# The second layer of an ffn by Strassen's seven products, with buffers turned in place, in a fused attention and ffn kernel

## The chip, the cores and the metric

The kernel runs on one core of a Trainium2 chip. The metric is the device time of one execution in microseconds; the kernel before takes 1520.41 us (median of 3 runs, 1520.29 to 1524.58). All arithmetic is in fp32.

## The reference

Attention with a threshold for 8 batches of 8 heads, 576 tokens and 64 columns a head; its output, 4608 rows of 512 columns, goes into a feed-forward network (ffn) with two first-layer weights whose products are multiplied element by element.

```python
scores = scale * np.matmul(q, k.transpose(0, 1, 3, 2))        # q, k, v: (8, 8, 576, 64)
thresh = np.max(scores, axis=-1, keepdims=True) - tau
scores = np.where(scores >= thresh, scores, -1000000000.0)
scores = scores - np.max(scores, axis=-1, keepdims=True)
attn = np.exp(scores)
attn = attn / (np.sum(attn, axis=-1, keepdims=True) + 1e-09)
x = np.matmul(attn, v)           # then (B, H, S, D) -> (B*S, H*D) = (4608, 512)
a = x @ w_a                      # w_a, w_b: (512, 1536), float64 in memory
b = x @ w_b
return (a * b @ w_out)           # w_out: (1536, 512)
```

## The kernel before

The work of attention is cut into 160 units: a pair of heads with 128 rows of each (or, at the end of a pair, the last 64 rows of both). The ffn is cut into 18 blocks of 256 rows. TensorE's program interleaves them: after the scores of a unit come pieces of the current ffn block, counted in columns, so that TensorE has work while VectorE and ScalarE do the softmax. All engines run their instructions in the order written. Every matmul uses a quarter of the array (64 rows by 64 columns), so that four run side by side; `r` picks the half of the rows and `c` the half of the columns.

Scores and softmax of a unit (`banks` gives a PSUM tile of two banks; there are four):

```python
    def scores(i, u):
        ...                                    # matmuls into sc[0], sc[1], 128x576 each
        for j in range(n):
            c = slice(j, j + 1)
            nc.vector.tensor_reduce(mx[:, c], sc[j], axis=AX.XY, op=ALU.max)
            nc.gpsimd.tensor_scalar(bias[:, c], mx[:, c], e_nscale, None, op0=ALU.mult)
        nc.gpsimd.tensor_scalar(thr[:, 0:n], mx[:, 0:n], cut, None, op0=ALU.subtract)

    def weigh(i, u):
        for j, s in enumerate(sc):
            w = work.tile([P, S], FP32, tag="w", bufs=W_BUFS, name="w")
            nc.scalar.activation(..., s, AF.Exp, bias=bias[:, j:j + 1], scale=e_scale)
        for j, s in enumerate(sc):
            nc.vector.scalar_tensor_tensor(out=wv, in0=s, scalar=thr[:, j:j + 1], in1=wv,
                op0=ALU.is_ge, op1=ALU.mult, accum_out=sums[:, j:j + 1])
```

The weights are normalised by ScalarE, turned in 32x32 blocks by VectorE into another tile `tb`, and written to a scratch buffer in HBM and read back turned (`wT`). q and k are loaded into tiles `qm`, `km` and turned by VectorE into `qT`, `kT`:

```python
    def turn_blocks(i, u):
            for j, w in enumerate(ws):
                nc.vector.transpose(tb[...], w.rearrange("p (n e) -> p n e", e=Q))
            for g in range(G):
                nc.sync.dma_start(swap[...], tb[g * Q:(g + 1) * Q])
    def prep(i, name):
        mT = work.tile([P, S], FP32, tag=name + "T", bufs=HP, name=name + "T")
        nc.vector.transpose(mT, m.rearrange("p n e -> p (n e)"))
```

The weighted values go into the tile `xT`; GpSimd copies its upper and lower halves crosswise into `xS`:

```python
    def exchange(x, xs, hp, c0, c1, engine):
        for r in range(2):
            engine.tensor_copy(xs[r * D:(r + 1) * D, hp, c0:c1], x[(1 - r) * D:(2 - r) * D, hp, c0:c1])
    def join(out, lo, hi):
        nc.scalar.copy(out, lo)
        nc.vector.tensor_tensor(out, out, hi, op=ALU.add)
```

One block of the ffn (`HALF` is 256, `NF` 12, `DM` 512, `H` 8); each `yield` is a place where attention may come in between:

```python
    def ffn(xT, what):
        for f, c0, c1 in steps:                     # first layer: 6 steps of 256 hidden columns
            for w in (wa_sb, wb_sb):
                pab = banks(c1 - c0, "pab")
                for k in range(H):
                    for r in range(2):
                        for c in range(2):
                            nc.tensor.matmul(pab[c * D:(c + 1) * D, r],
                                             w[rows, f // n, k, fs + c * D:fs + (c + 1) * D], moving,
                                             start=(k == 0), stop=(k == H - 1))
                    yield ...
                if w is wa_sb:
                    nc.scalar.copy(ht, pab)
                else:
                    nc.vector.tensor_tensor(ht, ht, pab, op=ALU.mult)
        for u in range(2):                          # second layer: 128 rows at a time
            po = banks(DM, "po")
            for F in range(NF):
                for r in range(2):
                    for c in range(2):
                        nc.tensor.matmul(po[c * D:(c + 1) * D, r], ht[rows, t0:t0 + D], wo_sb[rows, F, :],
                                         start=(F == 0), stop=(F == NF - 1))
                yield ...
            join(osb, po[:, 0], po[:, 1])
            pending.append((out[r0:r0 + P, :], osb))
```

At the start the float64 weights are loaded and turned into fp32 by ScalarE, GpSimd and VectorE, in 36 pieces.

Of the kernel before, what the change touches and what calls it, by code (L numbers as in the profile page):

```python
# [11 lines left out]
U32 = mybir.dt.uint32  # L12
# [12 lines left out]
XT_BUFS = 7  # L25
W_BUFS = 4
# [7 lines left out]
PORTIONS = (0.3, 0.35, 0.15, 0.2)  # L34

# [15 lines left out]
def kernel(  # L51
# [81 lines left out]
    def load(i, name, engine=nc.sync):  # L133
# [3 lines left out]
        t = loads.tile([P, NB, Q], FP32, tag="qk", bufs=3, name=name + "m")  # L137
# [45 lines left out]
    raws, stages, extra = {}, {}, []  # L183
    state = {"loaded": 0, "converted": 0, "rows": 0}

    def load_weights(limit, engine=nc.sync):

        while (len(raws) < limit or extra) and state["loaded"] < NPIECES:
            n = state["loaded"]
            if len(raws) < limit:  # L190
                raw = work.tile([P, CW, 2], U32, tag="xT", bufs=XT_BUFS, name="raw")
            else:
                raw = extra.pop(0)
# [34 lines left out]
    def convert_sign(n):  # L228
        if n in stages:
            low, hi = stages[n].bitcast(U32), raws.pop(n)[:, :, 1]  # L230
            nc.vector.scalar_tensor_tensor(out=low, in0=hi, scalar=0x80000000, in1=low,  # L231
                                           op0=ALU.bitwise_and, op1=ALU.bitwise_or)

# [14 lines left out]
    rooms = []  # L248
    for _ in range(2):
        t = work.tile([P, 2 * NB, 2 * Q], FP32, tag="tb", bufs=2, name="rows")  # L250
        t = t.rearrange("p n e -> p (n e)")[0:R]
        rooms += [t[:, c:c + 2 * NR * D].rearrange("p (n w) -> p n w", n=NR)
                  for c in range(0, 6 * NR * D, 2 * NR * D)]
# [10 lines left out]
    for name in ("q", "k"):  # L264
        t = work.tile([P, CW, 2], FP32, tag="xT", bufs=XT_BUFS, name="rows")
        t = t.rearrange("p n e -> p (n e)")[0:R, 0:2 * NR * D]
        load_rows(3, name, t.rearrange("p (n w) -> p n w", n=NR))
# [19 lines left out]
    def prep(i, name):  # L287

        m = loaded[i][name]
        mT = work.tile([P, S], FP32, tag=name + "T", bufs=HP, name=name + "T")  # L290
        nc.vector.transpose(mT, m.rearrange("p n e -> p (n e)"))
# [16 lines left out]
    def scores(i, u):  # L308
# [14 lines left out]
        for j in range(n):  # L323
            c = slice(j, j + 1)
            nc.vector.tensor_reduce(mx[:, c], sc[j], axis=AX.XY, op=ALU.max)  # L325
            nc.gpsimd.tensor_scalar(bias[:, c], mx[:, c], e_nscale, None, op0=ALU.mult)  # L326
        nc.gpsimd.tensor_scalar(thr[:, 0:n], mx[:, 0:n], cut, None, op0=ALU.subtract)  # L327
        scored[i, u] = (sc, thr, bias)

    def weigh(i, u):  # L330

        sc, thr, bias = scored.pop((i, u))
        n = len(sc)
        sums = small.tile([P, 2], FP32, tag="sums", name="sums")
        ws = []
        for j, s in enumerate(sc):
            w = work.tile([P, S], FP32, tag="w", bufs=W_BUFS, name="w")
            nc.scalar.activation(w.rearrange("p (c k) -> p c k", c=2), s, AF.Exp, bias=bias[:, j:j + 1], scale=e_scale)  # L338
            ws.append(w)
        for j, s in enumerate(sc):  # L340
            wv = ws[j].rearrange("p (c k) -> p c k", c=2)
            nc.vector.scalar_tensor_tensor(  # L342
                out=wv, in0=s, scalar=thr[:, j:j + 1], in1=wv,
# [27 lines left out]
    def turn_pe(i, u):  # L371

        ws, dg = weights.pop((i, u))
        wT = work.tile([P, NSLOT, P], FP32, tag="wT", bufs=WT_BUFS, name="wT")
# [24 lines left out]
    def turn_blocks(i, u):  # L399

        ws, _ = weights.pop((i, u))
        if u < NT:
            if u % 2 == 0:
                tbufs[i] = work.tile([P, 2 * NB, 2 * Q], FP32, tag="tb", bufs=2, name="tb")
            tb = tbufs[i]
            for j, w in enumerate(ws):
                nc.vector.transpose(  # L407
                    tb[:, j * NB:(j + 1) * NB, (u % 2) * Q:(u % 2 + 1) * Q],
                    w.rearrange("p (n e) -> p n e", e=Q))
# [10 lines left out]
        else:  # L420
            tb = work.tile([P, S], FP32, tag="w", bufs=W_BUFS, name="tbt").rearrange("p (n e) -> p n e", e=Q)
            nc.vector.transpose(tb.rearrange("p n e -> p (n e)"), ws[0])
# [95 lines left out]

    def ffn(xT, what):
# [9 lines left out]
        for f, c0, c1 in steps:  # L529
            while (state["converted"] < 2 * HP * (f // n + 1)  # L530
                   or kind == "first" and state["rows"] * P < c1):
                yield 0, 0
# [223 lines left out]
```

## Time and profile before

| What | Value |
|---|---|
| time, median of 3 | 1520.41 us |
| profiled execution, first to last instruction | 1516.9 us |
| TensorE (PE) busy | 1461.7 us |
| VectorE (DVE) busy | 848.3 us |
| ScalarE (ACT) busy | 587.8 us |
| GpSimd (POOL) busy | 262.3 us |
| TensorE's granted clock, mean | 0.994 |
| 16 DMA engines, mean rate | 146 GB/s |

In the page, a row of the groups names line, engine, operation and tiles, then how often, the busy time of the group, the mean duration of one, and the idle time of the engine just before them with what ended most of it. A matmul of fp32 stands in the trace as two records, so 1728 matmuls of the second layer are 3456 records. PEld is the load of the stationary operand, which runs beside matmuls. Busy times of TensorE's groups overlap where two groups alternate, so they don't add up to the engine's total. The row of slices cuts the span in 40 parts and gives each part's busy share in tenths.

### The profile page before, as it was taken

The numbers are of one execution on the slowest core, as the hardware profiler recorded it, in microseconds if no ns is written. First come the engines' busy times: TensorE is split into PE (matmuls) and PEld (weight loads), VectorE is DVE, ScalarE is ACT, GpSimd is POOL, SyncE is SP. The second block draws the span as 40 slices with busy tenths as digits, with TensorE's granted clock in tenths as the row PEclk, the third lists the DMA queues.
The fourth block names the chain that finished last, engine by engine and source line by source line (L and its number), as shares of the span: only waits on it lengthen the run. The fifth ranks groups of instructions, "written<-read, shape, count | busy, mean of one in ns | idle before, by whom it ended". The sixth has DMA issues, their size and how long they took to land.

```text
span 1516.9 us, 51632 instructions
## 1 busy us (share of the span) xinstructions
PE 1461.7 (96%) x22896; PEld 1139.6 (75%) x22896; DVE 848.3 (56%) x1838; ACT 587.8 (39%) x929; POOL 262.3 (17%) x662
## 2 busy tenths in 40 slices
PE   6777999999999999999999999999999999999998
PEld 4666586786978587778877887777877978687775
DVE  5667676667656765675545755576646665510000
ACT  4766344444443443443333433343433443410000
POOL 2766211111110111020100101011111111110000
PEclk9999999999999999999999999999999999999999
DMA  9858888788868976796547966588748876530000
GB/s 204 177 149 217 174 164 192 179 160 192 193 148 159 192 182 150 145 195 144 123 106 146 195 145 145 124 173 176 183 90 162 184 180 132 123 75 16 2 16 15
DMA packets 625839, 220.93 MB, mean 146 GB/s; under 512 B 543184, under 2 KB 613328, under 8 KB 625616
## 3 DMA queue, kind: packets, MB, share of 16 engines
q1 hardware_dynamic: 623248, 217.04, 65.2%
q8 instruction: 180, 2.95, 0.8%
q10 hardware_dynamic: 2368, 0.59, 0.2%
q14 instruction: 43, 0.35, 0.1%
HBM read 127.40 MB, written 89.65 MB: 143 GB/s over the span
## 4 chain that ended last, share of the span: by engine, by line
PE 85%; DVE 4%; SPq 4%; DMA 3%; ACT 2%; issue 1%; POOL 0%; DVEq 0%; ACTq 0%; POOLq 0%
PE pab L544 45%; PE po L564 22%; PE sc L318 9%; PE pv L455 9%; SPq L417 2%; SPq L142 1%; DVE mx L325 1%; SPq L429 1%; DVE tb L407 1%; PE tp L380 1%; DVE low L231 0%; DVE w L342 0%; DMA swap<-tbt 0%; DMA wT<-swap 0%; DMA xS<-xT 0%
## 5 line engine op out<-in xcount | busy, mean ns | idle before, releaser
L564 PE MATMUL po<-wo_sb,h 64*64 64x512 f32 x3456 | 423.2, 589 | 0.0
L325 DVE TENSOR_REDUCE mx<-sc 128x1 f32<-128x576 f32 x288 | 205.1, 749 | 220.2 <-PE sc L318 213.8
L564 PEld LDWEIGHTS po<-wo_sb,h 64*64 64x64 f32 x3456 | 225.4, 133 | 130.5 <-issue 72.8
L338 ACT ACTIVATE w<-sc,bias,scalars 128x576 f32<-128x576 f32 x288 | 226.9, 827 | 186.7 <-POOL bias L326 181.4
L544 PE MATMUL pab<-xS,wa_sb 64*64 64x256 f32 (+1 forms) x3584 | 277.7, 370 | 4.4 <-POOL xS L465 3.3
L544 PE MATMUL pab<-xS,wb_sb 64*64 64x256 f32 (+1 forms) x3584 | 277.1, 371 | 0.5 <-issue 0.5
L361 ACT ACTIVATE w<-w,rcp 128x576 f32<-128x576 f32 x272 | 197.7, 768 | 182.0 <-DVE rcp L355 182.0
L326 POOL TENSOR_SCALAR bias<-mx,scalars 128x1 f32<-128x1 f32 x288 | 90.3, 316 | 1022.3 <-DVE mx L325 616.8
L318 PE MATMUL sc<-kT,qT 64*64 64x288 f32 x2304 | 249.8, 413 | 16.2 <-DVE kT L306 7.5
L544 PE MATMUL pab<-xT,wb_sb 64*64 64x256 f32 (+1 forms) x3200 | 248.3, 369 | 5.5 <-DVE h L552 3.9
L544 PE MATMUL pab<-xT,wa_sb 64*64 64x256 f32 (+1 forms) x3200 | 245.7, 370 | 4.1 <-POOL thr L327 2.1
L342 DVE SCALAR_TENSOR_TENSOR w<-sc,thr,w 128x576 f32<-128x576 f32 x288 | 222.4, 804 | 18.5 <-ACT w L338 15.8
L544 PEld LDWEIGHTS pab<-xS,wa_sb 64*64 64x64 f32 x3584 | 193.7, 133 | 36.8 <-POOL xS L465 10.1
L544 PEld LDWEIGHTS pab<-xS,wb_sb 64*64 64x64 f32 x3584 | 196.3, 134 | 28.2 <-issue 2.0
L544 PEld LDWEIGHTS pab<-xT,wa_sb 64*64 64x64 f32 x3200 | 174.6, 134 | 30.7 <-issue 3.3
L544 PEld LDWEIGHTS pab<-xT,wb_sb 64*64 64x64 f32 x3200 | 175.7, 133 | 27.9 <-DVE h L552 4.4
L455 PE MATMUL pv<-wT,vm 64*64 64x320 f32 (+3 forms) x2592 | 190.0, 381 | 5.6 <-ACT h L550 2.8
L318 PEld LDWEIGHTS sc<-kT,qT 64*64 64x64 f32 x2304 | 146.6, 135 | 56.6 <-issue 14.1
L407 DVE STREAM_TRANSPOSE tb<-w 128x576 f32<-128x576 f32 x240 | 171.4, 752 | 1.3 <-ACT w L361 1.3
L455 PEld LDWEIGHTS pv<-wT,vm 64*64 64x64 f32 x2592 | 146.3, 135 | 32.7 <-issue 7.7
L552 DVE TENSOR_TENSOR h<-h,pab 128x512 f32<-128x512 f32 (+1 forms) x112 | 73.1, 653 | 132.8 <-PE pab L544 128.9
L550 ACT COPY h<-pab 128x512 f32<-128x512 f32 (+1 forms) x112 | 63.5, 567 | 200.1 <-PE pab L544 199.6
(62 smaller groups left out, 702.8 us busy)
## 6 DMA issues: line engine op xcount, KB each, us to landing
swap<-tb SPq DMA_DIRECT2D x240, 288.0 KB, 5.3
wT<-swap SPq DMA_DIRECT2D x28, 1440.0 KB, 7.3
wT<-swap SPq DMA_DIRECT2D x32, 1152.0 KB, 6.2
vm<-in_v_dram SPq DMA_DIRECT2D x32, 288.0 KB, 4.8
swap<-tbt SPq DMA_DIRECT2D x128, 72.0 KB, 2.8
out_dram<-osb SPq DMA_DIRECT2D x32, 256.0 KB, 5.0
qm<-in_q_dram SPq DMA_DIRECT2D x112, 72.0 KB, 3.5
km<-in_k_dram SPq DMA_DIRECT2D x112, 72.0 KB, 4.6
```

The costliest lines, as they stand in the source:

```text
L318: nc.tensor.matmul(sc[j if u < NT else 0][to, c], qT[r, q0:q0 + D], kT[r, c * SH:(c + 1) * SH], start=True, stop=True)
L325: nc.vector.tensor_reduce(mx[:, c], sc[j], axis=AX.XY, op=ALU.max)
L326: nc.gpsimd.tensor_scalar(bias[:, c], mx[:, c], e_nscale, None, op0=ALU.mult)
L338: nc.scalar.activation(w.rearrange("p (c k) -> p c k", c=2), s, AF.Exp, bias=bias[:, j:j + 1], scale=e_scale)
L342: nc.vector.scalar_tensor_tensor(out=wv, in0=s, scalar=thr[:, j:j + 1], in1=wv, op0=ALU.is_ge, op1=ALU.mult, accum_out=sums[:, j:j + 1])
L361: nc.scalar.activation(w, w, AF.Copy, scale=rcp[:, j:j + 1])
L407: nc.vector.transpose(tb[:, j * NB:(j + 1) * NB, (u % 2) * Q:(u % 2 + 1) * Q], w.rearrange("p (n e) -> p n e", e=Q))
L455: nc.tensor.matmul(pv[j * D:(j + 1) * D, r], vm[rows, k0], wT[rows, k0], start=(s == (NT if j == r else 0)), stop=(s == NT - 1))
L544: nc.tensor.matmul(pab[c * D:(c + 1) * D, r], w[rows, f // n, k, fs + c * D:fs + (c + 1) * D], moving, start=(k == 0), stop=(k == H - 1))
L550: nc.scalar.copy(ht, pab)
L552: nc.vector.tensor_tensor(ht, ht, pab, op=ALU.mult)
L564: nc.tensor.matmul(po[c * D:(c + 1) * D, r], ht[rows, t0:t0 + D], wo_sb[rows, F, :], start=(F == 0), stop=(F == NF - 1))
```

## The change

The second layer multiplies, for a block, a matrix of hidden values (256 rows of tokens by 1536) with `w_out` (1536 by 512). The change cuts each into two by two parts (two halves of tokens, two kinds of hidden chunks, two halves of the columns) and computes the product with seven products of half size instead of eight, in Winograd's form of Strassen's method. Four products need sums and differences of hidden values, three of them need sums of weights. The sums of weights (`t1`, `t2`, `t4`) are computed once and kept in SBUF; the sums of hidden values are written by GpSimd over the hidden values themselves, as soon as the product that reads the old value is done; the outputs are put together by GpSimd from the joined products. The first blocks, for which the sums of the weights are not ready, run the old way.

To make room in SBUF for the sums, q and k are turned in the tile they are loaded to, and the attention weights are written by ScalarE straight into the tile from which they are sent out and turned there; there are six x tiles for seven; the room of the sums serves as room for q, k and raw weights at the start. To free GpSimd, the bias of the exponential is computed by ScalarE and the threshold by VectorE, once the sums of the weights are ready. Raw weights are held in four x tiles throughout and in four places of the sums' room that are used again.

The core of the diff, with cuts marked:

```diff
-XT_BUFS = 7
-W_BUFS = 4
+XT_BUFS = 6
+RAWS = 4
...
-        t = loads.tile([P, NB, Q], FP32, tag="qk", bufs=3, name=name + "m")
+        t = work.tile([P, NB, Q], FP32, tag=name + "T", bufs=HP, name=name + "T")
...
-        mT = work.tile([P, S], FP32, tag=name + "T", bufs=HP, name=name + "T")
-        nc.vector.transpose(mT, m.rearrange("p n e -> p (n e)"))
+        mT = loaded[i][name].rearrange("p n e -> p (n e)")
+        nc.vector.transpose(mT, mT)
...
-            nc.gpsimd.tensor_scalar(bias[:, c], mx[:, c], e_nscale, None, op0=ALU.mult)
-        nc.gpsimd.tensor_scalar(thr[:, 0:n], mx[:, 0:n], cut, None, op0=ALU.subtract)
+            if not state["sums"]:
+                nc.gpsimd.tensor_scalar(bias[:, c], mx[:, c], e_nscale, None, op0=ALU.mult)
+        engine = nc.vector if state["sums"] else nc.gpsimd
+        engine.tensor_scalar(thr[:, 0:n], mx[:, 0:n], cut, None, op0=ALU.subtract)
...
+            state["tw"] = work.tile([P, 2 * NB, 2 * Q], FP32, tag="tw", bufs=2, name="tw")
...
+            if not biased:
+                nc.scalar.activation(bias[:, j:j + 1], mx[:, j:j + 1], AF.Copy, scale=e_nscale)
+            nc.scalar.activation(wb[j], sb[j], AF.Exp, bias=bias[:, j:j + 1], scale=e_scale)
...
-            for j, w in enumerate(ws):
-                nc.vector.transpose(
-                    tb[:, j * NB:(j + 1) * NB, (u % 2) * Q:(u % 2 + 1) * Q],
-                    w.rearrange("p (n e) -> p n e", e=Q))
+            for w in ws:
+                nc.vector.transpose(w, w)
...
+    def weight_sums(n, z):
+        f = slice(z * NG, (z + 1) * NG)
+        w = wo_sb.rearrange("p (f k) (c w) -> p f k c w", k=2, c=2)[:, f]
+        w11, w12, w21, w22 = (w[:, :, k, c] for k in range(2) for c in range(2))
+        t1, t2, t4 = (sums_of[:, f, m] for m in range(3))
+        out, a, b = ((t1, w12, w11), (t2, w22, t1), (t4, w21, t2), (w12, w22, w12))[n]
+        nc.gpsimd.tensor_tensor(out, a, b, op=ALU.subtract)
...
+        if state["sums"]:
...
+            seven = {1: (0, 0, w[:, :, 0, 0]), 4: (1, 1, t4), 2: (1, 0, w[:, :, 1, 0]), 5: (1, 1, t1),
+                     7: (0, 1, w[:, :, 0, 1]), 6: (0, 0, t2), 3: (1, 0, w[:, :, 1, 1])}
+
+            def h_sums(out, a, b, op):
+                for f in range(0, NG * n, 2):
+                    o, x1, x2 = (hs[f + k][:, :, u * P:(u + 1) * P] for k, u in (out, a, b))
+                    pool(o, x1, x2, op=op)
...
+            for both in ((1, 4), (2, 5), (7, 6), (3,)):
+                po = banks(len(both) * CH, "po").rearrange("p r (m w) -> p r m w", w=CH)
...
+                for y, m in enumerate(both):
+                    k, u, other = seven[m]
+                    for f in range(NF // 2):
+                        ht = hs[f // 2 * 2 + k][:, f % 2]
+                        for r in range(2):
+                            rows = slice(r * D, (r + 1) * D)
+                            for c in range(2):
+                                t0 = u * P + c * D
+                                nc.tensor.matmul(po[c * D:(c + 1) * D, r, y], ht[rows, t0:t0 + D],
+                                                 other[rows, f], start=(f == 0), stop=(f == NF // 2 - 1))
+                        left -= CH
+                        if m == 4 and f == NF // 2 - 1:
+                            h_sums((1, 1), (0, 1), (1, 1), ALU.add)
+                            h_sums((0, 1), (0, 0), (0, 1), ALU.subtract)
+                            h_sums((0, 0), (1, 1), (0, 0), ALU.subtract)
+                        if m == 2 and f == NF // 2 - 1:
+                            h_sums((1, 0), (1, 0), (0, 0), ALU.subtract)
+                        if left:
+                            yield CH, left, whole
+                if 3 not in both:
+                    t = keep("kept")
+                    join(t, po[:, 0], po[:, 1])
+                if 1 in both:
+                    k14 = t
+                elif 2 in both:
+                    k25 = t
+                    pool(k25[:, 0], k25[:, 0], k14[:, 0], op=ALU.add)
+                elif 7 in both:
+                    k76 = t
+                    pool(k76[:, 1], k76[:, 1], k14[:, 0], op=ALU.add)
+                    pool(k76[:, 0], k76[:, 0], k76[:, 1], op=ALU.add)
+                    pool(k14[:, 0], k76[:, 0], k14[:, 1], op=ALU.add)
+                    pool(k14[:, 1], k76[:, 0], k25[:, 1], op=ALU.add)
+                    pool(k76[:, 1], k76[:, 1], k25[:, 1], op=ALU.add)
+                    written(1, k14)
+                else:
+                    t = keep("kept")[:, 0]
+                    join(t, po[:, 0, 0], po[:, 1, 0])
+                    pool(k25[:, 1], k76[:, 1], t, op=ALU.add)
+                    written(0, k25)
+                yield CH, 0, 0
+            return
```

`CH` is 256 and `NF // 2` is 6, so a product is 24 matmuls of 256 columns.

## The prediction

> **What bounds the kernel now.** I read the engine totals first, then the forty slices, then the table of stages, then TensorE's rate where nothing but the ffn runs. From the page:
>
> ```profile
> PE 1461.7 (96%) x22896; PEld 1139.6 (75%) x22896; DVE 848.3 (56%) x1838; ACT 587.8 (39%) x929; POOL 262.3 (17%) x662
> ...
> PE   6777999999999999999999999999999999999998
> ```
>
> TensorE is busy in 96% of the span, and the missing part lies in the first four slices. The table of stages (busy time of each engine in a stretch) says the same with numbers:
>
> ```profile
> 100.00:150.00 50.00, 39.23 (x928) 32.27 (x932) 37.84 (x81) 31.83 (x55) 34.92 (x41) 0.96 0.73 209
> 150.00:200.00 50.00, 47.70 (x652) 30.51 (x648) 32.15 (x68) 20.04 (x33) 12.51 (x29) 0.97 0.83 170
> ...
> 300.00:600.00 300.00, 296.56 (x4575) 232.52 (x4571) 198.45 (x432) 129.04 (x194) 44.02 (x144) 1.00 0.79 172
> 600.00:900.00 300.00, 299.99 (x4721) 237.32 (x4717) 177.97 (x386) 116.14 (x177) 39.68 (x128) 1.00 0.71 152
> ```
>
> The columns are TensorE, its weight loads, VectorE, ScalarE, GpSimd. After 600 us TensorE has no gap at all. A busy TensorE need not be at its best, so I counted columns. In the groups of TensorE from 800 to 1000 us, the records times their columns are 946,016 for the 64x64 products; at the rate found below (0.2108 ns a column) that is 199.4 of 200 us. From 600 to 800 it is 198.6, from 400 to 600 it is 196.6, from 200 to 400 only 189.7. So from 400 us on, the time is TensorE's columns times a fixed rate, and a column taken away is time taken away. Before 200 us it isn't: there the loads, the conversion of the weights and the first softmax units set the pace.
>
> The rate by width, from the rows of costly groups and from the end of the run:
>
> ```profile
> L564 PE MATMUL po<-wo_sb,h 64*64 64x512 f32 x3456 | 423.2, 589 | 0.0
> ...
> L544 PE MATMUL pab<-xS,wa_sb 64*64 64x256 f32 (+1 forms) x3584 | 277.7, 370 | 4.4 <-POOL xS L465 3.3
> ```
>
> The first is the second layer, the other one of the groups of the first layer. The means (589 and 370 ns) mislead: each is one record with its latency, and four quarters of the array run side by side. The spacing counts. In the order of time of TensorE:
>
> ```profile
> 1366.10 0.59 PE L564 MATMUL po<-wo_sb,h 64*64 64x512 f32 x2
> ...
> 1386.70 0.60 PE L544 MATMUL pab<-xT,wa_sb 64*64 64x256 f32 x4
> ...
> 1395.34 0.38 PE L544 MATMUL pab<-xS,wa_sb 64*64 64x256 f32 x2
> ...
> 1397.06 0.38 PE L544 MATMUL pab<-xT,wb_sb 64*64 64x256 f32 x2
> ...
> 1398.79 0.38 PE L544 MATMUL pab<-xS,wb_sb 64*64 64x256 f32 x2
> ```
>
> The first number is the start. A group of 32 records of 256 columns begins every 1.726 us (the last three lines): 53.95 ns a record, 0.2108 ns a column. The second layer of one block, 192 records of 512 columns (96 matmuls, each recorded twice), lies between the first two lines, 20.60 us: 107.3 ns a record, 0.2096 ns a column. Halving the width costs 0.6% a column, no more.
>
> **What the Trainium skill says.** "TensorE: Matmul & The Clock Gate", in its part on packing small matmuls: weight loads are pulled ahead of running matmuls when they go to another row group. The trace agrees: at 256 columns a record comes each 54 ns although a weight load takes 133 ns, so twice as many loads in the second layer need not show. The same page's section on the back-to-back gap gives a small fixed cost a matmul (about 2.5 ns); the trace has 53.95 - 107.3/2 = 0.3 ns a record with four tiles side by side, and I use the trace. "GPSIMD Engine Reference", section on elementwise cycle accounting: an operation on two tensors costs GpSimd about 2.6 cycles an element, one on a single tensor far less. The trace has 1279 ns for 512 elements with two inputs (the add of the weight conversion), and 396 ns for a copy of 256. "SBUF — State Buffer", section on the two sides: GpSimd and VectorE exclude each other on one shared pair of ports, but only when VectorE reads two SBUF tensors or runs in a two-port mode. VectorE's large operations here read at most one tensor from SBUF and one from PSUM; nothing in the trace before tests it at this GpSimd load.
>
> **The change part by part.**
>
> *Columns on TensorE.* A block had 2 x 12 x 4 = 96 matmuls of 512 columns. It gets 7 x 6 x 4 = 168 of 256: 43,008 columns for 49,152, exactly 7/8. In records: 336 x 53.95 ns = 18.13 us for 20.60 us, 2.47 us less a block. The order of instructions of the changed kernel still has 96 matmuls of 512 columns, so one block of 18 runs the old way (the sums of the weights aren't ready), and 2856 = 17 x 168 of 256. 17 x 2.47 = 42.0 us less. All other TensorE work keeps its count.
>
> *Sums of the hidden tiles on GpSimd.* Twelve subtractions or additions of 128x256 a block. An estimate from the two rows above: about 180 ns fixed and 2.15 ns an element, so 0.73 us each. They are asked for after product 4 and used by product 5, after product 2 has given 24 x 2 x 53.95 ns = 2.6 us of cover; and product 5 waits for them in three steps, so the first 0.73 us is enough. All twelve take 8.8 us; the last ones are needed by product 3, 10.4 us after product 4 (four products). So they fit even with nothing else on TensorE, as in the last two blocks; in the middle the scores and the weighted values make more room. One copy of the halves of x (8 x 0.40 = 3.2 us) ahead of them in GpSimd's queue uses up most of the slack: a wait of about a microsecond in some blocks. Seven additions of 128x256 for the outputs (5.1 us) follow; nothing on TensorE waits for them.
>
> *GpSimd's total.* 17 x 19 x 0.73 = 236 us, and 15 us of sums of the weights (8 operations of 768 elements at the same rate); less 250 of the 288 biases (79 us) and 139 of the 160 thresholds (48 us). About 385 us, 26%.
>
> *VectorE and ScalarE.* VectorE gets 139 thresholds at some 155 ns (as the like operation on 128x2, 159 ns): 22 us. Its joins go from two of 512 columns a block to three of 512 and one of 256: 17 x (0.68 + 0.40) = 18 us. 848 becomes about 888 us, 60 to 61%. ScalarE gets 250 biases at some 205 ns, 51 us, and 17 x 0.95 = 16 us of joins: about 655 us, 44%. Neither reaches TensorE. The bias then follows the row maximum without a turn through GpSimd, at 205 for 316 ns.
>
> *Buffers.* q and k are turned in the tile they were loaded to, and the weights in the tile they were written to. The order in which they are asked for shows the margin: a tile of weights is written again four units later at the earliest, while its transfer out begins two units after its first use and lands in 5.3 us; a unit takes some 8 us. The tile of q for a new pair is loaded three to six units after the old pair's last scores. Six x tiles for seven: a tile handed out again had its last matmul earlier in TensorE's order than the product that refills it, so no wait follows.
>
> Sum: 1520.4 - 42.0 = 1478.4 us. What comes back: from 150 to 400 us TensorE had some 13 us of slack at this rate, set by VectorE's chain in units with two score tiles, so about half of the first two or three blocks' savings (3 us) is not got; and GpSimd's and PSUM's turns, about 1 us. I predict **1482 us**, a fall of 2.5%.
>
> **The rivals.**
>
> *GpSimd becomes the new wait.* The sums wait in order behind copies of x that themselves wait for VectorE. Against: 26% load, cover as above. For: order in the queue, and one shared port. One stop of 1.5 us in each of 17 blocks gives 26 us back: about 1505 us.
>
> *The attention chain becomes the bound.* VectorE had 63 of 100 us between 400 and 500 us, and gets more per unit while a unit gets shorter; in units with two score tiles it is far closer to full. PSUM is four tiles of two banks, two held by scores; a block now takes four output tiles for two, the last held by only 2.6 us of matmuls while the one before waits for a join of 1.3 us. For: those 200 to 400 us. Against: 600 us and later has no wait at all. It would give back 10 to 15 us: 1490 to 1495 us.
>
> *Half-width matmuls cost more than in the first layer.* The pairs of products and the moving operand in another tile change nothing that I can find; 5% more a record would be 0.9 us a block, 15 us: about 1495 us.
>
> *Something at the start gains.* Raw weights get four reusable places in the room of the sums, and biases stay on GpSimd there. TensorE's order is the same up to the 28th unit. A few microseconds either way.
>
> **Range and chances.** Low end: all 42.0 us and some 5 from the start, 1473. High end: half of a rival, 1497. The line of 2% is 1490.0 us, 8 above my number; the rivals that cross it have about a quarter together. Faster by over 2%: 0.76, within 2%: 0.22, slower: 0.02.
>
> **What would show it.** Right: the second layer's last two blocks take about 18.2 us of TensorE each; TensorE's busy time falls by about 42 us and stays at 96%; it stays at 10 of 10 after 600 us; the waits of TensorE on GpSimd stay under 5 us; GpSimd reads near 385 us, VectorE near 890, ScalarE near 655. Wrong: a row of TensorE waiting for the sums of h, with tens of microseconds; sums of 128x256 of over 1 us; records of the new matmuls more than 54 to 55 ns apart; gaps of TensorE between 200 and 600 us that are now larger than before.

## The result and the profile after

The changed kernel takes 1494.97 us (median of 4 runs, 1494.27 to 1495.72), the kernel before 1520.35 us (4 runs, 1517.19 to 1524.58): a ratio of 0.9831, interval 0.9807 to 0.9856. That is a fall of 1.7% where 2.5% was predicted, 25 us instead of 38. It lies inside the stated range (1473 to 1497 us), but does not reach the line of 2% (1490.0 us), to which the prediction gave a chance of 0.76. The profiled executions span 1492.9 us and 1516.9 us; all readings below are of these.

The engine totals and the forty slices of the changed kernel:

```profile
PE 1425.4 (95%) x25344; PEld 1214.9 (81%) x25344; DVE 905.3 (61%) x2011; ACT 669.7 (45%) x1213; POOL 395.5 (26%) x604
...
PE   5678899999999999999999999999999999999997
```

TensorE is busy 36.3 us less, not 42, and 95% instead of 96. The first five slices read 5678 and 8 where they read 6777 and 9, the last one 7 where it read 8. The table of stages of the changed kernel (busy time of TensorE, its weight loads, VectorE, ScalarE, GpSimd, then granted clock, DMA share, GB/s):

```profile
60.00:80.00 20.00, 9.62 (x168) 8.40 (x172) 6.45 (x16) 5.55 (x12) 6.20 (x8) 0.74 0.56 124
...
300.00:600.00 300.00, 295.57 (x5190) 259.07 (x5189) 213.87 (x485) 152.53 (x276) 61.53 (x102) 1.00 0.81 173
600.00:900.00 300.00, 298.55 (x5334) 262.48 (x5328) 194.55 (x434) 138.23 (x250) 62.29 (x102) 1.00 0.72 155
```

and of the kernel before, the one stage that was not shown:

```profile
60.00:80.00 20.00, 15.05 (x328) 12.96 (x326) 13.12 (x31) 14.39 (x30) 15.12 (x19) 0.99 0.59 140
```

From 60 to 80 us VectorE, ScalarE and GpSimd have lost half of their work or more, and TensorE runs 168 records for 328: all wait for something. (TensorE's busy time falls less, 9.62 us for 15.05, at a granted clock of 0.74 for 0.99.) From 600 to 900 us TensorE is idle for 1.45 us where it was idle for 0.01. The products themselves, in the order of time of TensorE, in a block where nothing else runs:

```profile
1347.30 0.41 PE L625 MATMUL po<-wo_sb,h 64*64 64x256 f32 x2
...
1349.89 0.41 PE L625 MATMUL po<-sums_u,h 64*64 64x256 f32 x2
...
1352.48 0.41 PE L625 MATMUL po<-wo_sb,h 64*64 64x256 f32 x2
...
1362.84 0.41 PE L625 MATMUL po<-wo_sb,h 64*64 64x256 f32 x2
...
1365.43 0.41 PE L584 MATMUL pab<-xT,wa_sb 64*64 64x256 f32 x2
```

A product of 48 records begins every 2.59 us (53.95 ns a record), and the seven take 18.13 us from the first line to the last. So the saving on TensorE's columns is there in full, and the missing time is time in which TensorE waits.

**Where it went.** To place the loss I took from both traces the start of the first scores of each of the 160 units (counted from 0), and subtracted what the columns issued up to there had saved at the measured rates. What remains is time lost, added up since the start; a negative number is time ahead. The columns are the kernel after and the main experiments:

| Lost against the kernel before, us, up to | after | E1 | E2 | E3 | E8 | E11 | E12 | E13 |
|---|---|---|---|---|---|---|---|---|
| unit 5 (50 us in the kernel before) | -1.9 | 0.0 | -3.8 | -3.9 | -3.6 | -3.4 | -0.3 | 0.3 |
| unit 6 (63 us) | 8.4 | 4.4 | 0.0 | 5.6 | -4.2 | 5.9 | -1.3 | -0.7 |
| unit 60 (481 us) | 10.1 | 7.3 | 3.3 | 2.5 | -3.2 | 9.5 | -6.0 | -6.6 |
| unit 100 (825 us) | 13.0 | 10.4 | 6.2 | 2.1 | -0.4 | 10.9 | -4.6 | -6.4 |
| start of TensorE's last matmul | 16.1 | 13.5 | 9.3 | 2.2 | 3.2 | 12.3 | -2.6 | -5.6 |

The first row has to be taken off before the runs are compared: up to unit 6 the changed kernel, E3 to E6, E9 and E11 run the same program, and yet their unit 5 begins anywhere between 46.0 and 50.6 us. A difference of a few microseconds between two medians below can be this alone; the differences between two rows of the table are free of it.

In the changed kernel 8.4 us are lost by unit 6 (10.3 between units 5 and 6, in the other six runs of the same start 9.3 to 10.1), 1.7 between there and unit 60, 6.0 from unit 60 to TensorE's end, and after that its end is 2.2 us longer (7.5 us from TensorE's end to the end of the program, 5.3 before). -42.1 + 16.1 + 2.2 = -23.8 us; the spans differ by 24.0.

*The start.* The waits of TensorE in the changed kernel (in total, times, longest):

```profile
PE pab L584 <- DMA xS<-xT: 9.5, 2, 5.4
...
PE pab L584 <- DVE kept L467: 2.1, 3, 1.0
```

The first was 1.1 us before. (Of the 10.3 us at most 1.1 can be the clock: the granted clock was half from 62.4 to 72.6 us, TensorE's wait ends at 69.33 and unit 6 begins at 71.5.) The issues of the DMA queue of SyncE show why (start, time for which the issues took, what is issued):

```profile
53.41 1.72 SPq L205 DMA_DIRECT2D raw<-in_moe_w_b_dram  x2
55.67 2.61 SPq L503 DMA_DIRECT2D xS<-xT  x2
58.39 1.33 SPq L205 DMA_DIRECT2D raw<-in_moe_w_a_dram  x2
59.83 1.26 SPq L205 DMA_DIRECT2D raw<-in_moe_w_b_dram  x2
61.60 1.71 SPq L205 DMA_DIRECT2D sums_u<-in_moe_w_a_dram  x2
63.36 1.25 SPq L503 DMA_DIRECT2D xS<-xT  x2
75.69 1.34 SPq L205 DMA_DIRECT2D sums_u<-in_moe_w_b_dram  x2
```

Three loads of raw weights of 512 KB each are issued from 58.39 us, and the small copy of x, for which the first block waits, behind them. Before the fourth of these copies 19 pieces of weights had been issued; in the kernel before it was 16. The four reusable places in the room of the sums do not count towards the limit of raw pieces, so the loads run ahead.

*Steady work.* The order of time of all engines of the changed kernel, around two of the gaps (in square brackets the idle time before and what ended it):

```profile
835.32 0.65 DVE L467 TENSOR_TENSOR kept<-kept,po 128x512 f32<-128x512 f32 x1
...
836.02 1.50 PEld L584 LDWEIGHTS pab<-xT,wa_sb 64*64 64x64 f32 x32 [0.36 <-DVE kept L467]
836.03 1.96 PE L584 MATMUL pab<-xT,wa_sb 64*64 64x256 f32 x32
...
837.36 0.78 DVE L296 STREAM_TRANSPOSE kT<-kT 128x576 f32<-128x576 f32 x1
...
838.19 1.18 PE L323 MATMUL sc<-kT,qT 64*64 64x288 f32 x13 [0.21 <-DVE kT L296]
```

Two different waits. At 836.02 the first layer of the next block waits for a PSUM tile until the join of products 7 and 6 has ended; product 3 alone covers that join with only 2.6 us. At 838.19 the first scores of a new pair begin 0.05 us after VectorE has turned k, an operation that stands behind the masking of the weights of the unit before. Between 240 us and the end there are five gaps of over 0.26 us of the first kind (3.6 us in all) and seven between first layer and scores (5.2 us). Four of the seven, 3.2 us, end within 0.1 us of the turn of k (502.2, 656.0, 838.2 and 1005.2 us), the other three 0.15 us after a masking by VectorE. Nine more gaps, 3.6 us in all, lie between the scores of one unit (two of 0.4 us in the kernel before); E3 below has nine with 2.8, so most of these come with the rest of the change and not with the seven products.

*The end.* The order of time of VectorE and GpSimd after TensorE's last matmuls in the changed kernel:

```profile
1483.59 0.69 DVE L467 TENSOR_TENSOR kept<-kept,po 128x512 f32<-128x512 f32 x1 [4.50 <-ACT kept L466]
1484.36 0.73 POOL L646 TENSOR_TENSOR kept<-kept 128x256 f32<-128x256 f32 x1 [4.15 <-DVE kept L467]
1485.16 0.72 POOL L647 TENSOR_TENSOR kept<-kept 128x256 f32<-128x256 f32 x1
...
1487.45 0.72 POOL L650 TENSOR_TENSOR kept<-kept 128x256 f32<-128x256 f32 x1
...
1488.25 0.72 POOL L655 TENSOR_TENSOR kept<-kept 128x256 f32<-128x256 f32 x1
```

TensorE has ended at 1485.47; GpSimd's six additions go on in series until 1488.97 us.

### The profile page after: what moved, and what is told of

Read it like the earlier page. It is cut to its first block, busy times and chain, and to the rows that moved or that the text cites. A ratio compares the mean times of both kernels' runs of the same rounds, so it can differ in the third digit from the quotient of the medians.

```text
span 1492.9 us, 57138 instructions
## 1 busy us (share of the span) xinstructions
PE 1425.4 (95%) x25344; PEld 1214.9 (81%) x25344; DVE 905.3 (61%) x2011; ACT 669.7 (45%) x1213; POOL 395.5 (26%) x604
## 4 chain that ended last, share of the span: by engine, by line
PE 86%; DVE 4%; DMA 3%; ACT 2%; SPq 2%; issue 2%; POOL 1%; ACTq 0%; POOLq 0%; DVEq 0%
PE pab L584 46%; PE po L625 19%; PE sc L323 10%; PE pv L477 9%; PE po L669 1%; DMA swap<-tw 1%; DVE mx L330 1%; DMA raw<-in_moe_w_b_dram 1%; DVE tw L431 1%; SPq L439 1%; DVE tw L365 1%; DMA sums_u<-in_moe_w_a_dram 1%; SPq L205 1%; PE tp L404 1%; ACT tw L362 1%
## 5 line engine op out<-in xcount | busy, mean ns | idle before, releaser
L606 POOL TENSOR_TENSOR h<-h 128x256 f32<-128x256 f32 x204 | 142.7, 734 | 633.5 <-PE po L625 629.7
L584 PE MATMUL pab<-xS,wa_sb 64*64 64x256 f32 (+1 forms) x3584 | 273.3, 372 | 10.4 <-DMA xS<-xT 9.5
L584 PE MATMUL pab<-xS,wb_sb 64*64 64x256 f32 (+1 forms) x3584 | 267.8, 371 | 0.0
L584 PE MATMUL pab<-xT,wb_sb 64*64 64x256 f32 (+1 forms) x3200 | 237.4, 372 | 5.5 <-DVE h L592 3.9
L625 PE MATMUL po<-wo_sb,h 64*64 64x256 f32 x3264 | 240.6, 376 | 0.0
L384 ACT ACTIVATE tw<-tw,rcp 128x576 f32<-128x576 f32 x244 | 176.1, 768 | 131.2 <-DVE rcp L378 131.1
L362 ACT ACTIVATE tw<-sc,bias,scalars 128x576 f32<-128x576 f32 x260 | 214.9, 832 | 43.8 <-POOL bias L332 26.6
L365 DVE SCALAR_TENSOR_TENSOR tw<-sc,thr,tw 128x576 f32<-128x576 f32 x260 | 203.9, 803 | 24.6 <-ACT tw L362 23.6
L625 PEld LDWEIGHTS po<-wo_sb,h 64*64 64x64 f32 x3264 | 178.7, 132 | 22.5
L625 PE MATMUL po<-sums_u,h 64*64 64x256 f32 x2448 | 180.8, 376 | 0.0
L431 DVE STREAM_TRANSPOSE tw<-tw 128x576 f32<-128x576 f32 x240 | 171.6, 753 | 0.2 <-ACT tw L384 0.2
```

The lines of the kernel that those rows point to most:

```text
L362: nc.scalar.activation(wb[j], sb[j], AF.Exp, bias=bias[:, j:j + 1], scale=e_scale)
L365: nc.vector.scalar_tensor_tensor(out=wv, in0=sb[j], scalar=thr[:, j:j + 1], in1=wv, op0=ALU.is_ge, op1=ALU.mult, accum_out=sums[:, j:j + 1])
L384: nc.scalar.activation(w, w, AF.Copy, scale=rcp[:, j:j + 1])
L431: nc.vector.transpose(w, w)
L584: nc.tensor.matmul(pab[c * D:(c + 1) * D, r], w[rows, f // n, k, fs + c * D:fs + (c + 1) * D], moving, start=(k == 0), stop=(k == H - 1))
L606: pool(o, x1, x2, op=op)
```

## The experiments

Each is the changed kernel with one edit, unless said otherwise. Ratios are against the kernel before.

**E1: the copies of x are issued first.**

```diff
+        exchange_dma()
         load_weights(RAWS)
```

> The changed kernel, but in each unit of the start the copies of x's halves (xS<-xT) are put into SyncE's queue ahead of that unit's weight loads. In the changed kernel 19 pieces of weights (512 KB each) are queued ahead of the fourth copy, in the kernel before 16, here 16 again. Theory (queue): the 8.8 us lost between units 5 and 6 come back, 1486 to 1488 us, and TensorE's wait for DMA xS<-xT (9.5 us) falls to 2 us or less. Rival (the copies are slow because all 16 DMA engines are full, in whatever order they are queued): 1494 to 1496 us. Rival (the start is hidden later by slack): the gap at 60 us goes and the total stays within 2 us of 1495.

1490.42 us (1488.04 to 1492.83), ratio 0.9795 (0.9771 to 0.982). The pieces issued ahead of the copies fall from 8, 14, 16, 19 to 6, 8, 14, 16, the wait for the copy from 9.5 to 5.6 us where 2 or less was expected, and the loss between units 5 and 6 from 10.3 to 4.4 us. The order of issue is more than half of the loss at the start, not all of it.

**E2: pieces in the room of the sums count towards the limit, as all did before.**

```diff
-        while (len(raws) - len(taken) < limit or extra) and ...
-            if len(raws) - len(taken) < limit:
+        while (len(raws) < limit or extra) and ...
+            if len(raws) < limit:
```

> The changed kernel with the old rule for loading weights: a piece held in the room of the sums counts towards the limit, so that no new load is queued while four are held. 16 pieces of weights are then ahead of the fourth copy of x's halves, 14 ahead of the third (16 and 15 in the kernel before, 19 and 16 in the changed one), and the copies stand where they stood. Theory (the extra loads ahead of the copies cost the 8.8 us): TensorE's wait for DMA xS<-xT falls under 3 us and the sixth unit begins at 63 to 65 us (63.1 before, 71.5 changed); 1486 to 1489 us. Rival (the copies land late for another reason, for instance the rows' room or six x tiles): the sixth unit still begins after 68 us; 1493 to 1496 us.

1487.29 us (1484.79 to 1490.37), ratio 0.9792 (0.977 to 0.9813). Unit 6 begins at 63.1 us as in the kernel before, but unit 5 had begun 3.8 us early: between the two 3.8 us are still lost (10.3 in the changed kernel), and a wait for the copy is left, 3.2 us for 1.1 in the kernel before:

```profile
PE pab L584 <- DMA xS<-xT: 3.2, 1, 3.2
```

From unit 6 to TensorE's end 9.3 us are still lost (7.7 in the changed kernel). So the loads that run ahead are more than half of the loss at the start as well, and this loss is separate from the steady one. That the total at unit 6 comes out at 0.0 is luck of the run. E1 and E2 overlap in what they do; together (E8, E12 and E13 below) they leave no loss between units 5 and 6: those three runs gain 0.6 to 1.0 us there.

**E3: the old second layer, with all else of the change.** Neither the sums of the weights (the fourth, which the kernel writes over a part of `w_out`, included) nor the sums of h are made.

```diff
-        if state["sums"]:
+        if False:
-        return BLOCK_COLS - (NF // 2 * CH if state["sums"] else 0)
+        return BLOCK_COLS
```

> The changed kernel with the second layer of all blocks in the old form (two tiles of 12 times four matmuls of 512 columns) and without the sums of weights; buffers turned in place, bias on ScalarE, threshold on VectorE and the new order of loads stay. Theory: the start costs 8.5 us and the rest of these parts next to nothing, so 1520.4 + 8.5 = 1529 us, 1526 to 1531. Rival (the move of bias and threshold or the shared buffers cost what is lost after the start, some 7 us): 1534 to 1538 us. Rival (these parts by themselves are neutral): 1519 to 1522 us.

1525.21 us (1520.37 to 1528.27), ratio 1.0037 (1.0019 to 1.0056). At unit 6 5.6 us are lost (9.5 since unit 5), at the end 2.2. The turning in place, the six x tiles and the moved biases cost nothing in steady work, they gain 3.4 us; the rest of the change by itself costs the start. The steady loss comes with the seven products, and counted against this run it is 11 us and not 7.7. Their own worth, against this run, is 30 us by the medians and 27 by the profiled executions (this one was among the fastest of twelve).

**E4: bias and threshold stay on GpSimd throughout.**

```diff
-            if not state["sums"]:
+            if True:
                 nc.gpsimd.tensor_scalar(bias[:, c], mx[:, c], ...)
-        engine = nc.vector if state["sums"] else nc.gpsimd
+        engine = nc.gpsimd
```

> The changed kernel with bias and threshold on GpSimd throughout, as before the change. Theory (GpSimd then has sums and biases in one queue): exponentials wait behind the sums of a block, up to 9 us, so TensorE waits for scores: 1500 us or more. Rival (the longer row of small operations on ScalarE and VectorE is what costs the 7 us after the start): 1488 to 1491 us.

1504.57 us (1502.14 to 1505.31), ratio 0.9899 (0.9878 to 0.9921), some 10 us slower than the changed kernel. From unit 20 to the end TensorE loses 14.1 us for 8.1. The order of time of GpSimd in E4 shows a unit that meets the second layer:

```profile
692.88 2.10 POOL L606 TENSOR_TENSOR h<-h 128x256 f32<-128x256 f32 x3
694.93 0.73 POOL L643 TENSOR_TENSOR kept<-kept 128x256 f32<-128x256 f32 x1
695.64 0.54 POOL L332 TENSOR_SCALAR bias<-mx,scalars 128x1 f32<-128x1 f32 x2
```

VectorE has the row maxima of this unit at 693.63 us; the biases begin 2.0 us later, behind three sums of h and an addition, and the exponential only after them, at 696.81. In units without the second layer a bias begins as soon as its maximum is there. So the queue of GpSimd would have been a wait, and moving bias and threshold away avoids it.

**E5: the sums of h are left out on GpSimd**, so that later products multiply other values than they should.

```diff
-                    pool(o, x1, x2, op=op)
+                    pass
```

> The changed kernel without the twelve sums of hidden values a block on GpSimd (left out, so the output is not the reference's); the additions of products on GpSimd stay. Rival (TensorE waits for the sums on GpSimd): 5 us or more faster, 1490 us or less. Theory (the sums are covered by product 2; the loss in the second layer is PSUM's turn): within 1.5 us of the changed kernel, 1493.5 to 1496 us, with the same gaps of TensorE.

1492.96 us (1488.75 to 1495.53), ratio 0.9809 (0.9783 to 0.9836), which overlaps the changed kernel. The same five gaps of 3.6 us stand between second and first layer, and from unit 6 to the end 8.0 us are lost (7.7). TensorE does not wait for GpSimd's sums in the changed kernel.

**E6: the products in other pairs**, (1, 4), (2), (5, 7), (6, 3), so that the single product is not the last; nine additions for seven.

```diff
-            for both in ((1, 4), (2, 5), (7, 6), (3,)):
+            for both in ((1, 4), (2,), (5, 7), (6, 3)):
```

> The changed kernel with the seven products in other pairs: (1,4), (2), (5,7), (6,3) for (1,4), (2,5), (7,6), (3); the product that has an output tile for itself comes second and not last, and the outputs are put together accordingly with nine additions on GpSimd for seven. Theory (the short last tile leaves only 2.6 us for the join of the tile before, so that the next block waits for PSUM): the gaps of 0.3 to 1.4 us between the second layer and the next first layer go, 3 to 5 us, 1490 to 1492 us. Rival (the gaps come from VectorE's and ScalarE's added work, not from the short tile): within 1.5 us of 1495. Rival (product 5, now after product 2 alone, waits for GpSimd): slower, 1497 us or more.

1498.57 us (1495.99 to 1500.76), ratio 0.9848 (0.9825 to 0.9872): no gain, rather a loss. The gaps behind the last product are gone, but others appear. Two before the weighted values take 2.6 us, and product 5 waits once for a sum of h (355.5 us, 0.8 us). Inside the first layer ten spacings are long, 5.5 us in all, but eight of them (2.7 us) lie between 379.3 and 382.5 us, where the granted clock was half (379.2 to 382.6 us), and are no waits. The other two, at 289.6 and 377.2 us, are waits for GpSimd's copies of the halves of x:

```profile
PE pab L584 <- POOL xS L487: 3.0, 3, 1.2
```

The changed kernel has one of these three, of 0.9 us. In both new ones the copy began behind four additions of products that GpSimd had in its queue. So the time is that of the third forecast, GpSimd, but mostly by another wait than the one it named: the additions, two more a block, and where they stand. The loss falls before unit 60 (9.3 us between units 6 and 60, 1.7 in the changed kernel); from unit 60 on E6 loses 1.9 us where the changed kernel loses 6.0. That is what the theory of the short last tile asks for, but with the additions changed as well the run does not show it by itself.

**E9: a join is two copies by ScalarE**, in place of a copy and VectorE's addition. The addition of the second half is left out.

```diff
-                    join(t, po[:, 0], po[:, 1])
+                    nc.scalar.copy(t, po[:, 0])
+                    nc.scalar.copy(t, po[:, 1])
```

> The changed kernel with the joins of the seven products done by two copies on ScalarE; the addition of the second half on VectorE is left out, so the output is not the reference's. Theory (a second-layer tile is held in PSUM because its addition stands in VectorE's queue behind softmax work): TensorE's gaps of 0.3 to 1.4 us after the second layer, 5 of them with 3.6 us, go, and of the 4 us lost more between 600 and 1200 us half or more comes back; 1491 to 1493 us. Rival (the loss lies in the half-width matmuls themselves or in the change between them and the scores): no gap moves, 1494 to 1496 us.

1491.88 us (1491.62 to 1492.9), ratio 0.9822 (0.9805 to 0.9839). The gaps between second and first layer fall from five with 3.6 us to one with 1.2; those before scores rise from 5.2 to 7.1. The join is a real wait, but TensorE runs from it into the next one, before the scores. Of the 3.1 us between the medians most is not the edit's: from unit 6 to the last matmul 7.6 us are lost (7.7 in the changed kernel; 1.5 less after unit 60 and as much more before it), while by unit 6 it is 2.8 us ahead of the changed kernel, in a part that the edit does not touch.

**E8: E1 and E2 together, and the additions of products by VectorE for the blocks after the last unit.**

```diff
                     k25 = t
+                    if state.get("end"):
+                        pool = dve
```

> A version meant to be better: the old rule for loading weights, the copies of x's halves ahead of the unit's loads (14 pieces ahead of the fourth copy), and, once attention is through, the additions of products on VectorE instead of GpSimd. Theory: 8 to 9 us from the start, 2 us from the end: 1483 to 1486 us. Rival (start hidden by slack later): 1491 to 1494 us.

1480.48 us (1479.84 to 1484.46), ratio 0.9751 (0.9731 to 0.9772). At unit 6 it is 4.2 us ahead of the kernel before, 3.6 of them already at unit 5; between the two it gains 0.6 us where the changed kernel loses 10.3. From TensorE's end to the program's end it is 5.9 us for 7.5. Both ends are explained, and the 2.5% of the prediction are reached with the steady loss still there (7.4 us from unit 6 to TensorE's last matmul). That the time is below the 1483 us that were expected can be the early unit 5.

**E11 and E10: k of a new pair is loaded and turned one unit earlier**, beside q; E11 on the changed kernel, E10 on E8.

```diff
-            for name, d in (("q", 2), ("k", 1)):      # turned so many units ahead
+            for name, d in (("q", 2), ("k", 2)):
-            for name, d in (("q", 4), ("k", 3)):      # loaded so many units ahead
+            for name, d in (("q", 4), ("k", 4)):
```

> The changed kernel with nothing else than k of a new pair loaded and turned one unit earlier. Theory (the turn of k is the wait before the first scores of a pair): 3 to 5 us less than the changed kernel, 1490 to 1492 us, and the gaps between first layer and scores fall from 5.2 us to under 2. Rival (the wait only moves): 1494 to 1496 us.

> The version that undoes the two losses at the start and at the end (1480.5 us) with one more change: k of a new pair is loaded and turned one unit earlier, beside q. In the changed kernel seven gaps of TensorE between the first layer and the first scores of a pair cost 5 us, and three of them end 0.05 to 0.1 us after VectorE's turn of k, which stands last in the unit before. Theory (the turn of k is the wait): these gaps nearly vanish, 3 to 5 us less, about 1476 to 1478 us. Rival (the scores wait for their PSUM tile or for VectorE's work as such, and two turns of 0.77 us in one unit only move the wait): the gaps stay in number or come back at another place, 1479 to 1482 us.

E11 takes 1492.30 us (1490.9 to 1495.57), ratio 0.9813 (0.9789 to 0.9837); E10 1483.93 us (1480.18 to 1487.04), ratio 0.9755 (0.9729 to 0.978), no better than E8, and both above what the theory gave. Yet the gaps before scores are nearly gone, in both from 5.2 (E8: 4.4) to 0.9 us. What took much of that away is one new wait, in E11:

```profile
PE pv L477 <- DMA wT<-swap: 2.7, 1, 2.7
```

and the issues of SyncE in E11 show its cause:

```profile
348.06 2.95 SPq L142 DMA_DIRECT2D qT<-in_q_dram  x4
351.06 2.12 SPq L142 DMA_DIRECT2D kT<-in_k_dram  x4
353.28 0.44 SPq L462 DMA_DIRECT2D wT<-swap  x1
```

The turned weights are read back behind eight loads of q and k. In the changed kernel that issue came at 349.71 us, behind four, although by unit 40 E11 was 1.9 us ahead of it. By the table E11 loses 2.8 us from unit 60 on, where the changed kernel loses 6.0, and 3.6 for 1.7 between units 6 and 60. In E10 the clock adds to it: it was half from 206.9 to 210.3 us and from 353.7 to 357.1 us, right behind waits of 2.2 and 3.1 us.

**E12: E8 with k turned two units ahead, and loaded five ahead**, so that the loads of q and k fall into different units.

```diff
-            for name, d in (("q", 4), ("k", 3)):
+            for name, d in (("q", 4), ("k", 5)):
```

**E13: the same with the joins of E9**, so that the additions of the second halves are left out.

> The version that undoes the losses at the start and at the end (1480.5 us), with k of a new pair turned one unit earlier (two units ahead) and loaded two units earlier (five units ahead), so that the loads of q and k do not follow each other in one unit. Turning it earlier with both loads in one unit took the gaps before the first scores from 5.2 to 0.9 us, but TensorE then stood 3.3 us once (unit 43) for weights read back from the scratch buffer, whose transfer was issued behind eight loads of q and k. Theory (the loads in one unit made that wait): the wait at unit 43 goes, the gain before the scores stays, about 1476 to 1478 us. Rival (the weights come late there for another reason): 1480 to 1484 us, with the wait at unit 43 still there.

> The same, and the joins of the products of the second layer are two copies by ScalarE in place of a copy and an addition by VectorE (this leaves out the addition of the upper half of the rows, so the output is not the reference's). Theory (in steady work the loss is the turn of k and the join, side by side, and little else): 1 to 2 us below the run with the turn of k alone, and TensorE's drift against its column rate from 600 to 1200 us falls to that of the kernel before (5.8 us). Rival (a wait hidden behind these takes their place): the same time as the run with the turn alone.

E12 takes 1474.06 us (1472.11 to 1476.74), ratio 0.9697 (0.9672 to 0.9722), the fastest complete version. The wait at unit 43 is down to 0.6 us and the gaps before scores stay at 0.9. Against E8 it gains 5.7 us between units 6 and 60 and 3.0 after; 1.7 of the first is half a clock that E8 had from 98.1 to 101.5 us and E12 had not, and the rest before unit 60 is not taken apart. From 600 to 900 us TensorE (first column) stands 0.67 us for 1.45 in the changed kernel:

```profile
600.00:900.00 300.00, 299.33 (x5360) 258.33 (x5358) 196.27 (x432) 138.33 (x251) 66.41 (x108) 1.00 0.72 156
```

E13 takes 1470.92 us (1468.63 to 1472.06), ratio 0.9672 (0.9648 to 0.9697), 3.1 us below E12, more than the 1 to 2 expected. TensorE's drift against its column rate from 600 to 1200 us (the 600 us less the columns issued in them at the measured rates), a longer measure of the steady loss, is 5.8 us in the kernel before, 9.9 in the changed kernel, 7.1 in E11, 7.6 in E12, 8.7 in E9 and 5.4 in E13; E1, E2, E5 and E8, which leave steady work as it is, come within 0.2 us of the changed kernel. With the turn of k and the join both out of the way the seven products run from 600 to 1200 us with no more loss than the old second layer.

## Why the prediction was right and where it was off

The mechanism was right: TensorE's columns set the time, and a column less is time less. The size was off by 13 us (38 predicted, 25 measured). By its steps:

- *Columns.* Predicted 2.47 us a block, 42.0 us. Confirmed: 18.13 us a block, at 53.95 ns a record. The rival of dearer narrow matmuls falls.
- *The sums of h.* Predicted 0.73 us each and covered by the products. Confirmed: 734 ns, and leaving them out (E5) moves no gap. The rival of GpSimd as the new wait falls for the kernel as changed; E4 shows that the move of the biases is what keeps it away.
- *Loss from 150 to 400 us, 3 us.* About right: 1.7 us between units 6 and 60 against the kernel before, 4.8 against E3.
- *"GpSimd's and PSUM's turns, about 1 us".* This term failed: 6.0 us from unit 60 on. The prediction wrote that the last output tile is held by only 2.6 us of matmuls while the one before waits for a join, and put that into a rival for 200 to 400 us alone, because "600 us and later has no wait at all". But a trace without waits shows no margin. There a join had had 10.3 us of matmuls beside it (half of 20.60) and has 2.6 now, and the turn of k had fitted. The change put more on VectorE (905.3 us for 848.3) and shortened the units; which of the two made the turn late is not settled. E9 and E11 to E13 show that these two waits, taken away together, are the loss from 600 to 1200 us (9.9 to 5.4 us of drift, 5.8 in the kernel before); E13 leaves the addition out, so it does not tell VectorE's queue from VectorE's work.
- *The start, "a few microseconds either way".* This term failed most: 10.3 us between units 5 and 6, where the sum had nothing. "TensorE's order is the same up to the 28th unit" is true and was not the point: the order of the DMA queue is what changed, by the four uncounted places for raw weights. Counting them (E2) gives back 6.5 us of it, issuing the copies first (E1) 5.9, and both together all.
- *The end.* "Nothing on TensorE waits for them" is true of the additions, but in the last block the output does: 2.2 us, which the sum lacked.
- *Engines.* GpSimd 395.5 us for 385, VectorE 905.3 for 888, ScalarE 669.7 for 655. The additions of products were sized right (729 ns); the small operations weren't: 257 ns a threshold for 155, 287 ns a bias for 205. That is 139 x 0.10 + 250 x 0.08 = 34 us of work on engines that are not the bound.
- *What would show it.* The waits of TensorE on GpSimd stayed under 5 us, as foreseen. From 600 to 900 us TensorE stands 0.5% of the stage, where none was expected, and the sign named for "wrong" came too: between units 20 and 60 (184 to 481 us) it lost 2.1 us more than before.

The rival of the attention chain and PSUM, with 10 to 15 us given back and 1490 to 1495 us, named the right total for a partly wrong reason: half of what came back came from the start.

## What to carry to other kernels

When a change frees buffers for loads, follow the order of the DMA queue as well as that of the engines: a small transfer that work waits for belongs ahead of the loads, and prefetch needs a limit. A trace without waits shows no margin: list what ended just in time (here a join and a turn at the end of a unit) before the bound engine is made faster. And count the serial work behind the last matmul apart from work that is hidden in the middle.

## What the runs showed of the hardware

Small operations of VectorE on SBUF lengthen beside GpSimd. The operations on `thr` by VectorE in the changed kernel (how many, shortest, median and longest in ns, first and last start, forms):

```profile
L334 DVE TENSOR_SCALAR thr<-mx,scalars x139: 212/228/846, 205.0 to 1306.5; 128x2 f32<-128x2 f32 x111, 128x1 f32<-128x1 f32 x28
```

and those on `sums`:

```profile
L378 DVE RECIPROCAL rcp<-sums x160: 150/166/168, 18.0 to 1309.6; 128x2 f32<-128x2 f32 x128, 128x1 f32<-128x1 f32 x32
L376 DVE TENSOR_SCALAR sums<-sums x144: 109/162/1030, 171.2 to 1309.4; 128x2 f32<-128x2 f32 x112, 128x1 f32<-128x1 f32 x32
```

113 thresholds that overlap no operation of GpSimd have a mean of 226 ns (213 to 231), the 26 that overlap one have 395 ns, up to 846; 11 of the 26 are not lengthened. The operation on `sums` of 1030 ns began in an operation of GpSimd of 1.8 us and ended with it. The reciprocals, as small, and 65 of the 160 beside GpSimd, never change. The Trainium skill, "SBUF — State Buffer", section on the two separate sides, says that GpSimd and some operations of VectorE (with two inputs from SBUF, or in a two-port mode) share one pair of ports as a lock, held for a whole instruction; and "VectorE: DVE Perf Modes", section on what auto-detection checks, that an operation with one source and its destination in SBUF may run in such a mode. The trace agrees for the thresholds and sums; the reciprocals, also of one source, show no such lock. It agrees for two inputs as well, in the order of time of VectorE at the end of E12:

```profile
1460.40 0.77 DVE L645 TENSOR_TENSOR kept<-kept 128x256 f32<-128x256 f32 x1
...
1465.58 0.42 DVE L648 TENSOR_TENSOR kept<-kept 128x256 f32<-128x256 f32 x1
```

The first began while GpSimd was at its last sum of h (until 1460.89 us), the second ran alone. Alone, VectorE needs 0.42 us for an addition that takes GpSimd 0.73. The prediction had named the shared ports and held them harmless because VectorE's large operations read PSUM; the small ones do not. In time it is little here: without the sums of h (E5) the thresholds on two columns fall from 268 to 232 ns, and no gap of TensorE with them.
